# A 2:4-pruned matrix product on one core: the first weights in one load, and the order of the first x tiles

## The chip, the core and the metric

The kernel runs on one core of a Trainium2 chip. A core has five engines with instruction streams of their own: TensorE (PE in the profile, its weight loads PEld), VectorE (DVE), ScalarE (ACT), GpSimd (POOL) and SyncE (SP). Data comes in and goes out by DMA; here SyncE and ScalarE issue all transfers, each on a queue of its own, and the rows SPq and ACTq of the timeline are those issues. The metric is the time of one execution in microseconds on the device. Before the change the median of three runs was 232.76 us (232.62 to 232.90).

## The reference

```python
B, S, D = 16, 512, 1024            # x: B x S x D, w: D x D, b: D, all bfloat16
wg = w.reshape(D // 4, 4, D)
mag = jnp.abs(wg)
order = jnp.argsort(mag, 1)
thr = jnp.take_along_axis(mag, order[:, 2:3, :], 1)
mask = (mag >= thr).astype(w.dtype)
wp = (wg * mask).reshape(D, D)
return jnp.einsum("bsd,df->bsf", x, wp) + b
```

Of every four neighbouring weights of a column those below the second largest magnitude are set to zero; then 8192 rows of x are multiplied by the pruned 1024 x 1024 matrix and the bias is added.

## The kernel before

x has 64 tiles of 128 rows (t = 0 to 63). A product with TensorE needs x with the reduction along the partitions, that is, transposed. Most tiles come transposed from the DMA (`load_lead`, `load_low`, `load_nat`). For the first seven (NPK = 7) the lower half of the reduction (k below 512) is done otherwise, since at the start there is neither a pruned weight nor time to wait for one in its final layout:

- The weights are loaded with the four members of a pruning group side by side on one partition (`w_sb`, `load_w`, line 100), in six pieces (`pieces`, line 130): pieces 0 to 3 are 256 columns each of the first half of the rows (g = 0), pieces 4 and 5 are 512 columns each of the second.
- VectorE prunes a piece in steps (`Piece.do`, line 164): `abs`, the larger and smaller of pairs (`hi`, `lo`), the second largest (`t1`, `t2`, `thr`), `mask`, and the multiplication into `wp` (`mult`). Steps may be cut into parts; in the names of the order below, u, v, s, t are single members of the group, x and y pairs of them, p and q halves of the columns. `mult0yp` is thus the first quarter of piece 0 to be ready, `mult2t` a quarter of piece 2. For pieces 2 and 3 ScalarE takes over the `abs` step (`abs2`, `abs3`).
- The seven tiles of x come in natural layout (`load_x`, line 103: tiles 5-6, 3-4, 2 and 0-1, 512 columns each), are transposed on TensorE (`transpose`, line 188, the `T` names; matmuls of line 193) and copied out of PSUM by ScalarE (`copy_xt`, line 196, the `C` names).
- TensorE then multiplies them piece by piece (`mm_piece`, line 213, the `M` names: M3.0yp is tile 3 with the quarter yp of piece 0; line 229). Sums of finished pieces are staged in SBUF by ScalarE (`stage`, the `S` and `U` names).

Meanwhile `wp` is spread into the layout of the later products (`spread`, line 144, the `W` names, into `wp_nat`), four DMAs for each half of the columns and of the rows. Tiles 7 to 11 start on the lower half of k (`open_solo`, `open_nat`, names E and A), all twelve are closed with the upper half (`closes`, line 423, `close`, line 451), and the other 52 follow in seven batches (line 472), eight products for each half of the columns, VectorE adding the bias out of PSUM (`evac`, line 435) and ScalarE's queue storing.

The order on each engine is written by hand (`order`, line 266): `run` (line 391) takes each engine's names in turn, emitting one as soon as what it needs has been emitted, and `seq` fixes the order of emission on the engine. TensorE's list begins with

```python
"T3a T4a T5a T6a T2a M3.0yp M4.0yp M3.0yq M4.0yq M5.0y M6.0y M3.0u M4.0u ..."
```

so tiles 3 and 4 are transposed first, then 5 and 6, then 2, and the first product waits for `mult0yp`. VectorE's list begins with `abs0a abs0b` (two members of the group each) and goes through pieces 0 to 5 without anything else between. SyncE's list, `W0.0 Z W0.1 X1 W1.0p X2 Y1 Y0 W1.1`, mixes spreads with loads of weights, bias and transposed x.

Ahead of all this TensorE runs matmuls on constants whose result nobody reads (`filler`, line 136; called in lines 404 and 405): six of 512 columns and fourteen of 128.

The loads that open the kernel stand in lines 118 to 129. The first weights (piece 0, 256 KB) are split: members 0 and 1 on SyncE's queue, 2 and 3 on ScalarE's. Behind them ScalarE's queue loads x tiles 5-6, SyncE's x tiles 3-4, x tile 2, piece 1, x tiles 0-1 and the further weights. `LATE` (lines 46, 492 and 494) is the number of last tiles that are stored in two halves, each as soon as its half of the columns is done, rather than whole.

Of the kernel before, what the change touches and what calls it, by code (L numbers as in the profile page):

```python
# [11 lines left out]
def kernel(  # L12
# [30 lines left out]
    STG = 8  # L43
    SOLO = 6
    GROUPS = ((0, 3), (3, 6), (6, 7))
    LATE = 6
    sizes = (4, 8, 8, 8, 8, 8, 8)
    batches = []
    t0 = NPK + LEAD
# [23 lines left out]
    def pe(i):  # L73
        return seq("pe", i)
# [4 lines left out]
    def act(i):  # L79
        return seq("act", i)  # L80
# [15 lines left out]
    def issue(eng, out_, in_):  # L96
        q = nc.sync if eng == "sp" else nc.scalar
        return seq(eng, q.dma_start(out_, in_))

    def load_w(g, c0, c1, ma=0, mb=4, eng="sp"):  # L100
        issue(eng, w_sb[:, g, ma:mb, c0:c1], wv[:, g, ma:mb, c0:c1])

    def load_x(ta, tb, eng="sp"):
        xs = const.tile([P, tb - ta, HK], bf16, name=f"x_{ta}")
        issue(eng, xs[:], xf[ta * P:tb * P, :HK].rearrange("(t p) k -> p t k", p=P))
        for t in range(ta, tb):
            x_sb[t] = xs[:, t - ta, :]
# [7 lines left out]

    xnat, held = {}, {}

    load_w(0, 0, 256, 0, 2)
    load_w(0, 0, 256, 2, 4, "act")
    load_x(5, 7, "act")  # L120
    act(nc.scalar.activation(spark[:], nc.const_aps.tensor(1.0, [P, 1], bf16), Act.Abs))
    load_x(3, 5)
    load_x(2, 3)
    load_w(0, 256, 512)
    load_x(0, 2)
# [10 lines left out]
    def filler(n, rep=1):  # L136
        for _ in range(n):
            pe(nc.tensor.matmul(warm_ps[:, :rep * P], lhsT=nc.const_aps.tensor(1.0, [P, P], bf16),  # L138
                                rhs=nc.const_aps.tensor(1.0, [P, rep * P], bf16), start=True, stop=True))
# [251 lines left out]
    def run(queues):  # L391
        while any(queues.values()):
            moved = False
            for eng, toks in queues.items():
                while toks and all(n in written for n in needs(eng, toks[0])):
                    emit(eng, toks[0])
                    tok = toks.pop(0)
                    written.add(tok)
                    if tok[0] == "M" or tok[0].islower():
                        written.update(atoms(tok))  # L400
                    moved = True
            assert moved, queues

    filler(6, 4)
    filler(14)
    run({eng: order[eng].split() for eng in order})

    def load_nat(ta, tb):
# [26 lines left out]
    def evac(o, ps, c0, c1, add=None):  # L435
        if add is None:
            dve(nc.vector.tensor_tensor(o[:, c0:c1], ps, bias_sb[:, c0:c1], op=Alu.add))  # L437
        else:
            dve(nc.vector.tensor_tensor(o[:, c0:c1].rearrange("p (n c) -> p n c", n=2),  # L439
                                        ps.rearrange("p (n c) -> p n c", n=2), add, op=Alu.add))  # L440
# [4 lines left out]
    def store(eng, t, o, c0=0, c1=Dout):  # L445
        issue(eng, rows(t)[:, c0:c1], o[:, c0:c1])
# [25 lines left out]
    for bi, (tb, nb) in enumerate(batches):  # L472
        if bi:
            load_batch(bi + 1)
        for j in range(nb):
# [9 lines left out]
            else:  # L485
# [4 lines left out]
                for h in range(2):  # L490
                    evac(o, pss[h][:], h * FH, (h + 1) * FH)
                    if t >= NT - LATE:
                        store("act", t, o, h * FH, (h + 1) * FH)
                if t < NT - LATE:
                    store("act", t, o)
# [30 lines left out]
```

## Time and profile before

| | |
|---|---|
| median of the runs | 232.76 us |
| the profiled execution | 232.89 us |
| its span, first to last instruction | 231.1 us |
| TensorE busy | 226.6 us, 98% of the span |
| VectorE busy | 107.9 us, 47% |
| ScalarE busy | 14.0 us, 6% |
| GpSimd busy | 17.6 us, 8% |

Times in the rows count from the first instruction. A row of the timeline has start, duration, engine, line, operation, what is written and read, the shapes and the number of like instructions that were merged; in brackets the idle time ahead of it and what ended it. A merged row's duration runs to the end of its last instruction; matmuls and VectorE's operations overlap their neighbours a little. A line "DMA to landing" gives the time from the issue of a transfer until its data are in place. A row of the windows gives, after the busy times, the granted clock of TensorE, the mean busy share of the DMA engines and what they moved in GB/s.

### The profile page before, as it was taken

The page shows a single profiled execution, that of the slowest core. Times are in us where ns is not written, and L with a number is a line of the kernel's source. Part 1 is how long each engine was busy: PE and PEld are TensorE (multiplying, and loading weights), DVE is VectorE, ACT ScalarE, POOL GpSimd, SP SyncE. Part 2 cuts the span into 40 slices and gives each one's busy share as a digit, 9 for nine tenths or more (in the row PEclk, how much of TensorE's full clock was granted, in tenths as well). Part 3 has the DMA queues.
Part 4 walks back from the last instruction along what each step waited for, and adds up shares of the span by engine and source line. Part 5 has one row for each costly group of instructions (what it writes and reads, how often), then busy time and mean ns, then how long its engine had stood idle before and what let it go on. Part 6 is the DMA issues. An engine that isn't in the chain of part 4 may idle for free.

```text
span 231.1 us, 2851 instructions
## 1 busy us (share of the span) xinstructions
PE 226.6 (98%) x1142; PEld 110.9 (48%) x1162; DVE 107.9 (47%) x200; ACT 14.0 (6%) x27; POOL 17.6 (8%) x15
## 2 busy tenths in 40 slices
PE   8999999999999999999999999999999999999995
PEld 5986444444444444444444444444444444444443
DVE  3999877844424424424424424423423423433434
ACT  2874100000000000000000000000000000000000
POOL 1000199700000000000000000000000000000000
PEclk9999999999999999999999999999999999999999
DMA  6999999997399422991259821693128932122122
GB/s 203 276 197 280 164 217 223 297 320 252 124 206 232 155 91 72 237 281 64 75 116 252 222 94 71 162 298 134 65 91 198 273 122 83 54 91 91 53 86 91
DMA packets 79308, 38.19 MB, mean 165 GB/s; under 512 B 64192, under 2 KB 71744, under 8 KB 79296
## 3 DMA queue, kind: packets, MB, share of 16 engines
q1 hardware_dynamic: 68384, 20.75, 43.6%
q10 hardware_dynamic: 10912, 17.27, 20.9%
q8 instruction: 9, 0.15, 0.3%
q14 instruction: 3, 0.02, 0.0%
HBM read 3.28 MB, written 16.78 MB: 87 GB/s over the span
## 4 chain that ended last, share of the span: by engine, by line
PE 98%; issue 0%; DVE 0%
PE ps L242 88%; PE ps L229 5%; PE tp L242 2%; PE ps L138 2%; PE tp L193 1%; PE ps L193 0%; DVE o L437 0%
## 5 line engine op out<-in xcount | busy, mean ns | idle before, releaser
L242 PE MATMUL ps<-wp_nat,xb 128*128 128x512 bf16 (+1 forms) x831 | 178.9, 375 | 0.9
L242 PEld LDWEIGHTS <-xb 128*128 128x128 bf16 x848 | 82.2, 98 | 97.7
L437 DVE TENSOR_TENSOR o<-ps,bias_sb 128x512 bf16<-128x512 f32 (+1 forms) x112 | 71.6, 677 | 113.7 <-PE ps L242 111.4
L433 POOL TENSOR_TENSOR st<-st,bias_sb 128x1024 f32<-128x1024 f32 x8 | 16.7, 2142 | 0.0
L242 PE MATMUL ps<-wp_nat,xlead 128*128 128x512 bf16 x63 | 14.7, 379 | 0.1
L242 PEld LDWEIGHTS <-xlead 128*128 128x128 bf16 x88 | 8.6, 98 | 10.2
L229 PE MATMUL ps<-wp,xt 128*128 128x256 bf16 (+1 forms) x130 | 12.8, 258 | 0.0
L439 DVE TENSOR_TENSOR o<-ps,st 128x512 bf16<-128x512 f32 x16 | 11.1, 691 | 2.8 <-PE ps L242 2.2
L229 PEld LDWEIGHTS <-xt 128*128 128x128 bf16 x130 | 10.9, 98 | 1.1
L242 PE MATMUL ps<-wp_nat,xlow 128*128 128x512 bf16 x47 | 10.6, 379 | 0.1
L264 ACT COPY st<-ps 128x512 f32<-128x512 f32 x14 | 7.4, 600 | 3.2 <-PE ps L229 3.1
L242 PEld LDWEIGHTS <-xlow 128*128 128x128 bf16 x48 | 4.7, 98 | 5.7
L159 DVE TENSOR_TENSOR mag<-mag,hi 128x256 bf16<-128x256 bf16 (+2 forms) x15 | 6.1, 435 | 0.1
L159 DVE TENSOR_TENSOR wp<-w_sb,mag 128x256 bf16<-128x256 bf16 (+2 forms) x15 | 6.1, 435 | 0.1
L242 PE MATMUL tp<-wp_nat,xlead 128*128 128x512 bf16 x23 | 5.8, 380 | 0.0
L138 PE MATMUL ps<-const-bfloat16-1.0 128*128 128x128 bf16 (+1 forms) x20 | 4.2, 408 | 0.8 <-PEq L510 0.8
L169 DVE TENSOR_SCALAR mag<-w_sb 128x512 uint16<-128x512 uint16 (+2 forms) x5 | 2.3, 473 | 3.5 <-DMA w_sb<-in_w_dram 3.5
L138 PEld LDWEIGHTS <-const-bfloat16-1.0 128*128 128x128 bf16 x20 | 2.3, 146 | 2.4 <-issue 2.4
L159 DVE TENSOR_TENSOR hi<-mag 128x512 bf16<-128x512 bf16 (+2 forms) x7 | 3.2, 458 | 0.1
L159 DVE TENSOR_TENSOR lo<-mag 128x512 bf16<-128x512 bf16 (+1 forms) x6 | 3.1, 509 | 0.0
L193 PEld LDWEIGHTS <-x 128*128 128x128 bf16 x28 | 2.3, 124 | 0.3 <-DMA x<-in_x_dram 0.2
L422 POOL COPY pruned<-wp 128x1 bf16<-128x1 bf16 x1 | 0.2, 187 | 26.7 <-DVE wp L159 26.7
(18 smaller groups left out, 18.8 us busy)
## 6 DMA issues: line engine op xcount, KB each, us to landing
out_dram<-o ACTq DMA_DIRECT2D x58, 256.0 KB, 2.4
wp_nat<-wp SPq DMA_DIRECT2D x14, 128.0 KB, 3.2
out_dram<-o ACTq DMA_DIRECT2D x10, 128.0 KB, 1.7
w_sb<-in_w_dram SPq DMA_DIRECT2D x2, 512.0 KB, 5.5
w_sb<-in_w_dram SPq DMA_DIRECT2D x3, 256.0 KB, 5.1
x<-in_x_dram SPq DMA_DIRECT2D x2, 256.0 KB, 4.3
x<-in_x_dram ACTq DMA_DIRECT2D x1, 256.0 KB, 4.0
bias_sb<-in_b_dram SPq DMA_DIRECT2D x1, 256.0 KB, 4.7
```

Source lines behind the costliest of these rows:

```text
L138: pe(nc.tensor.matmul(warm_ps[:, :rep * P], lhsT=nc.const_aps.tensor(1.0, [P, P], bf16), rhs=nc.const_aps.tensor(1.0, [P, rep * P], bf16), ...
L159: dve(nc.vector.tensor_tensor(out, a, b_, op=op))
L169: dve(nc.vector.tensor_single_scalar(mag.bitcast(u16), w_.bitcast(u16), 0x7FFF, op=Alu.bitwise_and))
L193: pe(nc.tensor.transpose(tp[:, m, :], xg[:, m, :], ident[:]))
L229: pe(nc.tensor.matmul(ps[:, c0 + d:c1 + d], lhsT=xpk[t][:, m, :], rhs=wp[:, g, m, c0:c1], start=(new and m == ms.start), stop=(left[key] = ...
L242: pe(nc.tensor.matmul(ps, lhsT=xt[:, kt - koff, :], rhs=wp_nat[:, kt, c0:c1], start=(kt == first), stop=(kt == last)))
L264: act(nc.scalar.copy(staged[(q, h)][:, at, :, :].rearrange("p t c -> p (t c)"), ps_open.pop(key)[:]))
L422: pool(nc.gpsimd.tensor_copy(out=pruned[:], in_=wp[:, 1, 3, Dout - 1:]))
L433: pool(nc.gpsimd.tensor_tensor(st[:], st[:], bias.to_broadcast([P, 2, 2, CW]), op=Alu.add))
L437: dve(nc.vector.tensor_tensor(o[:, c0:c1], ps, bias_sb[:, c0:c1], op=Alu.add))
L439: dve(nc.vector.tensor_tensor(o[:, c0:c1].rearrange("p (n c) -> p n c", n=2), ps.rearrange("p (n c) -> p n c", n=2), add, op=Alu.add))
```

## The change

```diff
-    LATE = 6
+    LATE = 7
...
-    load_w(0, 0, 256, 0, 2)
-    load_w(0, 0, 256, 2, 4, "act")
-    load_x(5, 7, "act")
+    load_w(0, 0, 256)
+    load_x(3, 5, "act")
     act(nc.scalar.activation(spark[:], nc.const_aps.tensor(1.0, [P, 1], bf16), Act.Abs))
-    load_x(3, 5)
+    load_x(5, 7)
     load_x(2, 3)
     load_w(0, 256, 512)
...
     filler(6, 4)
-    filler(14)
+    filler(10)
```

The weights of piece 0 are loaded whole, in one transfer, as the first on SyncE's queue. x tiles 3-4 are the first and only opening transfer of ScalarE's queue; tiles 5-6 take their place on SyncE's, behind the weights and ahead of tile 2. What follows on SyncE's queue is unchanged. There are ten short fillers instead of fourteen. One more tile, 57, is stored in two halves. The order lists of the engines are the same; in the built program the instructions of TensorE, VectorE and ScalarE stand in the same order as before, except for those named, and lines after the loads move up by one.

## The prediction

> **What bounds the kernel now.** I read the page's summary first, then the chain of waits, then the first 5 us of the timeline, where all of the change but one line lies.
>
> ```profile
> span 231.1 us, 2851 instructions
> PEclk9999999999999999999999999999999999999999
> PE 98%; issue 0%; DVE 0%
> PE ps L242 88%; PE ps L229 5%; PE tp L242 2%; PE ps L138 2%; PE tp L193 1%; PE ps L193 0%; DVE o L437 0%
> ```
>
> The chain that ends last is TensorE from end to end. Once the products run, nothing but a hole in TensorE's own sequence makes the kernel longer, and only an earlier first product makes it shorter. L138 is the fillers, L193 the transposes of x, L229 the first products. So the question is when L229 starts, and whether it stalls after that.
>
> ```profile
> 0.73 0.45 SPq L98 DMA_DIRECT2D w_sb<-in_w_dram  x1
> 0.74 0.50 ACTq L98 DMA_DIRECT2D w_sb<-in_w_dram  x1
> 0.77 4.21 PE L138 MATMUL ps<-const-bfloat16-1.0 128*128 128x512 bf16 x20 [0.77 <-PEq L510]
> 1.24 0.96 SPq L98 DMA_DIRECT2D x<-in_x_dram  x2
> 1.26 0.49 ACTq L98 DMA_DIRECT2D x<-in_x_dram  x1
> 3.50 0.49 DVE L169 TENSOR_SCALAR mag<-w_sb 128x512 uint16<-128x512 uint16 x2 [3.50 <-DMA w_sb<-in_w_dram]
> 4.96 0.14 PEld L193 LDWEIGHTS <-x 128*128 128x128 bf16 x2 [0.24 <-DMA x<-in_x_dram]
> ```
>
> Today the two weight halves go out first, one on each queue; x 3-4 (SyncE) and x 5-6 (ScalarE) follow half a microsecond later. Two engines wait: VectorE until 3.50 for the weights, TensorE's weight load 0.24 us at 4.96 for x 3-4. What the waits are worth shows at the other end, where TensorE takes up what VectorE made. In the following rows of TensorE, by start, the last four are the first products of pieces 0, 1, 2 and 3:
>
> ```profile
> 3.29 1.70 PE L138 MATMUL ps<-const-bfloat16-1.0 128*128 128x128 bf16 x14
> 4.96 1.04 PE L193 MATMUL tp<-ident,x 128*128 128x128 bf16 x8
> 5.80 0.72 PE L193 MATMUL ps<-ident,x 128*128 128x128 bf16 x8
> 6.35 0.39 PE L193 MATMUL tp<-ident,x 128*128 128x128 bf16 x4
> 6.58 0.22 PE L229 MATMUL ps<-wp,xt 128*128 128x128 bf16 x1
> 10.09 0.39 PE L229 MATMUL ps<-wp,xt 128*128 128x128 bf16 x4
> 13.18 0.38 PE L229 MATMUL ps<-wp,xt 128*128 128x256 bf16 x2
> 16.24 0.38 PE L229 MATMUL ps<-wp,xt 128*128 128x256 bf16 x2
> ```
>
> and these are the multiplications on VectorE that they need (mult0yp, mult1yp, mult2t, mult3t):
>
> ```profile
> 5.80 0.28 DVE L159 TENSOR_TENSOR wp<-w_sb,mag 128x256 bf16<-128x256 bf16 x1
> 9.29 0.28 DVE L159 TENSOR_TENSOR wp<-w_sb,mag 128x256 bf16<-128x256 bf16 x1
> 12.49 0.28 DVE L159 TENSOR_TENSOR wp<-w_sb,mag 128x256 bf16<-128x256 bf16 x1
> 15.49 0.28 DVE L159 TENSOR_TENSOR wp<-w_sb,mag 128x256 bf16<-128x256 bf16 x1
> ```
>
> End of a multiplication to start of its product: 6.08 to 6.58, 9.57 to 10.09, 12.77 to 13.18, 15.77 to 16.24: 0.50, 0.52, 0.41 and 0.47 us. VectorE has no other wait from 3.50 to the last multiplication, so what its start loses, all four lose. It is half a microsecond ahead of TensorE four times over, and no more.
>
> **The change, part by part.** *The weights in one load.* Before, 256 KB of weights were all that the DMA engines had at first; after, the same 256 KB share them with 256 KB of x 3-4, sent at the same moment on the other queue. When they land is not in the trace; I work it out from what was moved.
>
> ```profile
> 1.50:2.00 0.50, 0.50 (x2) 0.15 (x1) 0.00 (x0) 0.21 (x1) 0.00 (x0) 1.00 0.11 27
> 2.00:2.50 0.50, 0.50 (x3) 0.22 (x2) 0.00 (x0) 0.50 (x1) 0.00 (x0) 1.00 0.56 151
> 2.50:3.00 0.50, 0.50 (x3) 0.22 (x2) 0.00 (x0) 0.50 (x1) 0.00 (x0) 1.00 1.03 302
> 3.00:3.50 0.50, 0.50 (x5) 0.23 (x4) 0.00 (x0) 0.28 (x2) 0.00 (x0) 1.00 0.82 275
> 3.50:4.00 0.50, 0.50 (x7) 0.50 (x6) 0.50 (x3) 0.00 (x0) 0.00 (x0) 1.00 1.09 389
> 4.00:4.50 0.50, 0.50 (x8) 0.50 (x6) 0.50 (x3) 0.00 (x0) 0.00 (x0) 1.00 1.10 383
> 4.50:5.00 0.50, 0.50 (x6) 0.26 (x5) 0.50 (x5) 0.00 (x0) 0.00 (x0) 1.00 1.08 357
> DMA to landing us min/median/max: 2.7/2.8/2.9
> ...
> DMA to landing us min/median/max: 4.0/4.0/4.0
> ```
>
> The last number of a window is GB/s; half of each, summed, gives 89 kB moved by 2.5 us, 240 by 3.0, 377 by 3.5, 572 by 4.0, 763 by 4.5. The two landing lines are of the weight halves and of x 5-6. Both halves (262 kB) are through at 3.0 + 22/275 = 3.08 and the later has landed at 0.74 + 2.9 = 3.64: 0.56 us on top. All four transfers (786 kB) are through at 4.56 and x 5-6 has landed at 1.26 + 4.0 = 5.26: 0.70 on top. Weights and x 3-4 together (524 kB) are through at 3.5 + 147/389 = 3.88. The two halves of today, on two queues, landed within 0.2 us of each other, so the queues share; of two equal loads sharing, the weights end with the pair: 3.88 + 0.56 = 4.44. VectorE would start at 4.45 instead of 3.50: 0.95 us later. Bounds: 0.14 (weights served before x, landing like the later half today, 3.64) and 1.46 (landing only at 4.96, when x 3-4 is taken up now). I take 0.95, since the one pair of loads in the trace that left together was shared.
>
> The Trainium skill (DMA: Bandwidth & Descriptors, section Queues, rings and completion order) says that each DMA engine goes round between the queue rows that have work, a packet at a time; two loads on two queues then end together. By that rule the start slips by the 0.95 us above; without sharing, by 0.14. The landings of the two halves agree with the rule.
>
> *From VectorE to TensorE.* One stretch of VectorE can shrink:
>
> ```profile
> 9.47 1.06 ACT L162 ACTIVATE mag<-w_sb 128x1024 bf16<-128x1024 bf16 x1
> 10.14 0.43 DVE L159 TENSOR_TENSOR wp<-w_sb,mag 128x512 bf16<-128x512 bf16 x1
> 10.56 0.43 DVE L159 TENSOR_TENSOR lo<-mag 128x512 bf16<-128x512 bf16 x1
> ```
>
> lo2 starts 0.03 us after ScalarE's abs2 ends (9.47 + 1.06 = 10.53); without that wait it would overlap the multiplication ahead of it by some 0.08, as the other independent neighbours do (mult0yp starts at 5.80 and mult0yq 0.20 later, each taking 0.28). A VectorE that comes 0.95 later doesn't wait there: 0.07 won back from piece 2 on. The 0.03 is also my price of a hand-over. The products then start at
> - piece 0: 6.08 + 0.95 + 0.03 = 7.06, 0.48 later than today's 6.58;
> - piece 1: 9.57 + 0.98 = 10.55, 0.46 later;
> - piece 2: 12.77 + 0.91 = 13.68, 0.50 later;
> - piece 3: 15.77 + 0.91 = 16.68, 0.44 later.
> The largest, 0.50, stays, since TensorE has no hole later in which to lose it.
>
> *x 3-4 first, 5-6 behind the weights, four fillers fewer.* A short filler takes (5.80 - 4.96)/8 = 0.105, the step of the cold transposes behind it. Ten end at 3.29 + 1.05 = 4.34 instead of 4.76, and x 3-4 lands by 4.44. x 5-6 ends the same 786 kB as today, so about 5.26; x 2 and the next weights likewise have as many bytes ahead of them as before. Transposes: 3 and 4 from 4.45, 5 and 6 from 5.3 at 0.105 each until the clock steps up, 2 after them: done by about 6.33, against 6.58. That gain of 0.25 us lies under the wait for mult0yp until 7.06, and so is worth nothing; if VectorE were early, it would be the whole gain. Conversely x 3-4 may land 0.7 us later than I say before it costs anything. SyncE's queue issues as many transfers as before, the first of them of double length, ScalarE's one fewer; the table load behind it on ScalarE comes earlier, and its first use, a copy of a transpose, not before 4.9.
>
> *What VectorE's delay moves behind it.* The spreads of finished weights on SyncE's queue wait for the multiplications, and transposing loads queue behind them. The last spread is the tightest:
>
> ```profile
> 30.04 2.49 SPq L98 DMA_DIRECT2D wp_nat<-wp  x4
> DMA to landing us min/median/max: 3.0/3.0/3.0
> 28.15 0.59 PE L242 MATMUL ps<-wp_nat,xlead 128*128 128x512 bf16 x2
> 31.38 7.07 PE ps L242 x32
> ```
>
> The fourth is issued at about 30.04 + 3/4 x 2.49 = 31.9 and has landed 3.0 later, at 34.9. The closings begin at 28.15 (third row) and take 7.07/32 = 0.22 a product (last row, of the chain of waits). The first reader of the fourth spread is the fortieth of them (nine closings of four, then the fourth product of the tenth): 28.15 + 39 x 0.22 = 36.7. 1.8 us of cover against 0.9: costs nothing; were the cover gone, the 0.9 would come in place of the 0.50.
>
> *LATE 7.* One more output tile leaves in two halves, about 20 us before the end, on a ScalarE queue that has nothing else to do: between 0 and the 0.3 us of an issue, hidden; I take 0.
>
> **Sum.** +0.50. The profiled execution took 232.89 us, its span 231.1 and 1.8 around it: 233.39, span 231.6. The median, 232.76, is 0.13 lower: 233.26. I say 233.3.
>
> **The rivals.** *A, the weights go first.* Place: the DMA engines between 1.8 and 3.9 us. If SyncE's transfer is served ahead of ScalarE's, VectorE is late by only 0.14; products start at 6.33, set by the transposes, and piece 2 at 12.77 + 0.14 + 0.03 = 12.94 or a little sooner, 0.24 earlier than 13.18. Gain 0.25: 232.5. It decides below a delay of about 0.45 us: there the kernel is not slower. For it: SyncE's issue starts a hair before ScalarE's (0.73, 0.74). Against it: the halves' landings.
>
> *B, the clock.* The page's clock row stays at 9, yet the steps of the transposes show a slow and a fast TensorE: 8 from 4.96 to 5.80 (0.105 each), 8 from 5.80 to 6.35 (0.069 on average), 4 from 6.35 to 6.58 (0.058). The step up falls at about 6.0, 5.25 us after the first filler. Four fewer fillers, and a wait of 0.7 us ahead of the first product, could put it off. Counted anew from 7.06, between the 1.06 us that it took from 4.96 and the 5.25 from the first filler would run at half pace, costing half of that, 0.5 to 2.6; the middle, 1.6, gives 234.9. Against it: fillers and transposes still leave no hole over 0.3 us up to 6.0. The Trainium skill (TensorE: Matmul & The Clock Gate, section Part 4: PE-mode transpose) has it that transposes don't count as activity for the clock; by that, fewer fillers would put the step off as in B. The trace agrees only in part: the step falls among transposes.
>
> *C, the change doesn't do what it says.* The two don't move at the same moment: x 3-4 takes the engines first and the weights land when x 3-4 is taken up today, at 4.96. VectorE is 1.46 late, the products 1.46 - 0.45 = 1.0: 233.8. Only the longer issue of SyncE's transfer speaks for it.
>
> **How the numbers follow.** Forecast 0.62, A 0.22, B 0.08, C 0.08. The time is the forecast's. Its own range, from a delay of 0.75 to 1.15 and 0.15 for the measurement, is 232.9 to 233.6. For 8 in 10 it goes down to 232.4 (A and a little) and up to 234.0 (C and the low end of B). 0.2% is 0.47 us, about what a measurement can tell from none: 232.3 and 233.2. Slower: all of B and C and some two thirds of the forecast, 0.58. Faster needs A and more than its 0.25: 0.06. The rest, 0.36, is within.
>
> **What would show it.** Right: VectorE's first row at 4.3 to 4.6; transposes at about 4.4; a wait of TensorE before the first product, ended by VectorE, and that product at 7.0 to 7.1; the first product of piece 2 at 13.6 to 13.7; 0.5 us more at every later point. Wrong: VectorE starting before 3.95 (A), the 0.105 us steps lasting past 7 us (B), VectorE after 4.8 (C), or a TensorE wait on a spread after 20 us.

## The result, and the profile after

The changed kernel takes 233.35 us (median of seven runs, 233.17 to 233.66); the kernel before took 232.51 beside it (seven runs, 232.40 to 232.90). The ratio is 1.0033, 95% interval 1.0024 to 1.0043: slower by 0.8 us. The profiled execution took 233.46 us, its span is 231.7.

First the chain of waits of the changed kernel, from its page:

```profile
span 231.7 us, 2864 instructions
PE 96%; DMA 2%; DVE 1%; issue 0%
PE ps L241 88%; PE ps L228 5%; PE tp L241 2%; DMA w_sb<-in_w_dram 2%; DVE hi L158 0%; DVE lo L158 0%; DVE mag L168 0%; DVE mag L158 0%; DVE o L436 0%; PE ps L192 0%; PE tp L192 0%; DVE wp L158 0%
```

Before, the chain was TensorE from end to end, fillers included (L138). Now it goes back from the first products to VectorE and from there to the load of the weights: 2% of 231.7 us is the time from the issue of that load to its landing, and the fillers are gone from the chain. One line of the page thus says what has changed: who holds the first product.

The timeline of the first 5 us of the changed kernel, and the times to landing of x 3-4, of the weights and of x 5-6 (in this order):

```profile
0.73 0.68 SPq L98 DMA_DIRECT2D w_sb<-in_w_dram  x1
0.74 0.43 ACTq L98 DMA_DIRECT2D x<-in_x_dram  x1
1.48 1.10 SPq L98 DMA_DIRECT2D x<-in_x_dram  x2
4.36 1.02 PE L192 MATMUL tp<-ident,x 128*128 128x128 bf16 x8
4.50 0.49 DVE L168 TENSOR_SCALAR mag<-w_sb 128x512 uint16<-128x512 uint16 x2 [4.50 <-DMA w_sb<-in_w_dram]
...
DMA to landing us min/median/max: 2.7/2.7/2.7
...
DMA to landing us min/median/max: 3.7/3.7/3.7
...
DMA to landing us min/median/max: 3.8/3.8/3.8
```

VectorE starts at 4.50, 1.00 later than before. But the two loads that left together didn't end together: x 3-4 landed at 0.74 + 2.7 = 3.4, and the weights a full microsecond behind it, at 4.4 to 4.5. TensorE had no use for x that early: its fillers ran on, and the first transpose came at 4.36.

TensorE's rows that answer to those of before, then VectorE's multiplications and the two operations around lo2:

```profile
5.28 0.64 PE L192 MATMUL ps<-ident,x 128*128 128x128 bf16 x8
5.75 0.39 PE L192 MATMUL tp<-ident,x 128*128 128x128 bf16 x4
7.13 0.27 PE L228 MATMUL ps<-wp,xt 128*128 128x128 bf16 x2 [0.99 <-DVE wp L158]
10.64 0.39 PE L228 MATMUL ps<-wp,xt 128*128 128x128 bf16 x4
13.75 0.50 PE L228 MATMUL ps<-wp,xt 128*128 128x256 bf16 x3
16.82 0.38 PE L228 MATMUL ps<-wp,xt 128*128 128x256 bf16 x2
19.88 0.59 PE L241 MATMUL tp<-wp_nat,xlead 128*128 128x512 bf16 x2
```

```profile
6.79 0.28 DVE L158 TENSOR_TENSOR wp<-w_sb,mag 128x256 bf16<-128x256 bf16 x1
10.28 0.28 DVE L158 TENSOR_TENSOR wp<-w_sb,mag 128x256 bf16<-128x256 bf16 x1
13.41 0.28 DVE L158 TENSOR_TENSOR wp<-w_sb,mag 128x256 bf16<-128x256 bf16 x1
16.41 0.28 DVE L158 TENSOR_TENSOR wp<-w_sb,mag 128x256 bf16<-128x256 bf16 x1
...
10.02 1.06 ACT L161 ACTIVATE mag<-w_sb 128x1024 bf16<-128x1024 bf16 x1
...
11.14 0.42 DVE L158 TENSOR_TENSOR wp<-w_sb,mag 128x512 bf16<-128x512 bf16 x1
11.48 0.42 DVE L158 TENSOR_TENSOR lo<-mag 128x512 bf16<-128x512 bf16 x1
```

The half microsecond between VectorE and TensorE is used up: 7.07 to 7.13, 10.56 to 10.64, 13.69 to 13.75, 16.69 to 16.82. TensorE finished its transposes at 6.14 (0.6 us before the old ones ended, at 6.74) and stood idle for 0.99. lo2 now starts 0.08 ahead of the end of the multiplication (11.56) and no longer waits for abs2 (11.08): the 0.07 that the prediction counted on. The first product of the next stage (L241) is at 19.88 against 19.30 in the profile of before, and the spans differ by the same: 231.7 against 231.1.

The 0.58 of the two profiles is less than the 0.8 of the medians. The first experiments below ask what the loss is made of, the last ones why the two numbers differ.

### The profile page after: what moved, and what is told of

Its sections match the earlier page's. It is cut to its first block, busy times and chain, and to the rows that moved or that the text cites. A ratio compares the mean times of both kernels' runs of the same rounds, so it can differ in the third digit from the quotient of the medians.

```text
span 231.7 us, 2864 instructions
## 1 busy us (share of the span) xinstructions
PE 227.2 (98%) x1158; PEld 110.5 (48%) x1158; DVE 107.8 (47%) x200; ACT 14.0 (6%) x27; POOL 17.6 (8%) x15
## 4 chain that ended last, share of the span: by engine, by line
PE 96%; DMA 2%; DVE 1%; issue 0%
PE ps L241 88%; PE ps L228 5%; PE tp L241 2%; DMA w_sb<-in_w_dram 2%; DVE hi L158 0%; DVE lo L158 0%; DVE mag L168 0%; DVE mag L158 0%; DVE o L436 0%; PE ps L192 0%; PE tp L192 0%; DVE wp L158 0%
## 5 line engine op out<-in xcount | busy, mean ns | idle before, releaser
L241 PE MATMUL ps<-wp_nat,xb 128*128 128x512 bf16 (+2 forms) x848 | 179.8, 375 | 0.0
L241 PEld LDWEIGHTS <-xb 128*128 128x128 bf16 x848 | 82.4, 98 | 97.5
L241 PE MATMUL ps<-wp_nat,xlead 128*128 128x512 bf16 x64 | 14.8, 379 | 0.0
L241 PEld LDWEIGHTS <-xlead 128*128 128x128 bf16 x88 | 8.6, 98 | 10.2
L241 PE MATMUL ps<-wp_nat,xlow 128*128 128x512 bf16 x48 | 10.7, 379 | 0.0
L241 PEld LDWEIGHTS <-xlow 128*128 128x128 bf16 x48 | 4.7, 98 | 5.7
L241 PE MATMUL tp<-wp_nat,xlead 128*128 128x512 bf16 x24 | 6.0, 379 | 0.0
```

Of the source, the lines that this page charges most:

```text
L241: pe(nc.tensor.matmul(ps, lhsT=xt[:, kt - koff, :], rhs=wp_nat[:, kt, c0:c1], start=(kt == first), stop=(kt == last)))
```

## The experiments

All kernels were run beside the kernel before; ratios are to that, with 95% intervals. Its median over these runs was 232.6 us.

**The parts of the change.** The loads alone, with fourteen fillers and LATE 6:

```diff
-    LATE = 7
+    LATE = 6
...
-    filler(10)
+    filler(14)
```

> The three edits of the loads alone; fourteen short fillers and LATE 6 as before the change. Theory (the weights land a microsecond later, because x 3-4 is sent at the same moment, and VectorE passes that on): VectorE starts at 4.5, the fillers end at 4.8, the transposes follow at once and still end before 6.6, the first product waits for VectorE until 7.1, and the ratio to before is that of the whole change, 1.0025 to 1.0045. Rival (the four missing fillers, by a later clock step, or the seventh split store): the loss is gone, ratio 0.999 to 1.001, first product at 6.6 or earlier.

233.44 us, ratio 1.0035 (1.0023 to 1.0047). VectorE started at 4.21, the transposes ran from 4.78 to 6.79, the first product came at 6.85, right behind `mult0yp`. The loads alone cost as much as the whole change. The expected times were 0.3 us too late, since the weights landed earlier here (4.19) than in the profile of the changed kernel (4.47).

The rest alone, in the kernel before:

```diff
-    LATE = 6
+    LATE = 7
...
-    filler(14)
+    filler(10)
```

> The loads of before; only ten fillers and LATE 7. Theory: VectorE at 3.5, TensorE waits for x 3-4 from 4.35 to 4.96, first product between 6.1 and 6.6 depending on when the clock steps up, ratio 0.999 to 1.001. Rival (fillers and store are the loss): ratio 1.0025 or more, the cold 0.105 us steps of the transposes lasting past 6.6, or the last tiles leaving later.

232.99 us, ratio 1.0010 (1.0000 to 1.0021), at the upper end of what the theory expected and below the rival's 1.0025. In the profile VectorE started at 3.40, and yet the first product came at 6.75, 0.76 after `mult0yp`: the transposes went at the slow step until 6.6. And the split store alone:

```diff
-    LATE = 6
+    LATE = 7
```

> Of the change only LATE 7. Theory: the split store is hidden, ratio 0.999 to 1.001. Rival (the 0.33 us by which the kernel with ten fillers, LATE 7 and the old loads stood above before come from the split store): ratio 1.001 to 1.002 with the last store landing later after TensorE's end.

232.61 us, ratio 1.0005 (0.9994 to 1.0016): no effect that can be told from none, so the 0.10% of the rest, if it is real, belongs to the fillers. It isn't settled that it is real, nor that fewer fillers put the fast step off: in the profiles with ten fillers it came between 4.7 and 6.7, in those with fourteen between 3.6 and 6.3 (one kernel with ten, in which it came at 9.8, follows below).

**Why the weights land late.** The changed kernel with `load_x(3, 5)` on SyncE's queue, everything else equal:

```diff
     load_w(0, 0, 256)
-    load_x(3, 5, "act")
+    load_x(3, 5)
```

> The changed kernel with one edit: x 3-4 behind the weights on SyncE's queue instead of beside them on ScalarE's, so that every opening load is on one queue in the order weights, 3-4, 5-6, 2. Theory (a transfer whose issue ends first is served first, and the weights, whose issue takes 0.68 us, lost their place to x 3-4, whose issue takes 0.43): nothing overtakes the weights, VectorE starts at 3.4 to 3.8, x 3-4 lands at 4.2 to 4.6, first product at 6.1 to 6.4, ratio to before 0.998 to 1.000. Rival (one load on one queue is slow whatever stands beside it): VectorE at 4.1 or later, first product at 6.7 or later, ratio 1.001 or more.

232.93 us, ratio 1.0022 (1.0004 to 1.0040), neither as good nor as bad as expected. From the profile, VectorE's first row, the weights' time to landing, the first product and the first of L241:

```profile
3.84 0.49 DVE L168 TENSOR_SCALAR mag<-w_sb 128x512 uint16<-128x512 uint16 x2 [3.84 <-DMA w_sb<-in_w_dram]
...
DMA to landing us min/median/max: 3.1/3.1/3.1
...
6.47 1.92 PE L228 MATMUL ps<-wp,xt 128*128 128x128 bf16 x20
...
19.22 1.03 PE L241 MATMUL tp<-wp_nat,xlead 128*128 128x512 bf16 x4
```

With nothing beside it, the single load landed 3.1 us after its issue instead of 3.7. So of the one microsecond that VectorE lost, about two thirds (4.50 to 3.84) is what x 3-4 took away, and the last third (3.84 to 3.50) is the single load itself: the halves landed 2.7 and 2.9 us after their issue. The issue on SyncE's queue took 0.68 us for the whole load and 0.45 for a half. The 3.50 is the latest start in six profiles with the loads of before; in the other five VectorE started between 3.33 and 3.40, and against those the single load itself costs nearer 0.5 us.

The trace also records every DMA packet (here one run in memory, 512 B of weights or 1 KB of x) with its queue: q1 is SyncE's, q10 ScalarE's. These moved from 1.5 to 2.75 us, first in the changed kernel, then in `all_sp`, then in the kernel before:

```profile
q10 hardware_dynamic: 193, 0.20, 45.3%
...
q1 hardware_dynamic: 187, 0.10, 28.8%
...
q1 hardware_dynamic: 232, 0.12, 35.1%
q10 hardware_dynamic: 97, 0.05, 13.1%
```

In the changed kernel 193 of the 256 packets of x 3-4 had gone by then and none of the weights: their first packet went at 2.81, against 2.20 in `all_sp`, and these 0.61 us are nearly all of the 0.66 between the two starts of VectorE. So x 3-4 went first and the weights behind it. The engines were not full meanwhile: the packets of x took 45.3% of their time. The halves of the kernel before (first packets at 1.83 and 2.29) did overlap, with SyncE's ahead.

The other attempt to leave the weights alone failed in an instructive way. x 5-6 was put on ScalarE's queue behind the table load, to be sent late:

```diff
-    load_x(3, 5, "act")
     act(nc.scalar.activation(spark[:], nc.const_aps.tensor(1.0, [P, 1], bf16), Act.Abs))
-    load_x(5, 7)
+    load_x(5, 7, "act")
+    load_x(3, 5)
```

> The weights whole on SyncE's queue as in the change, but nothing beside them: x 3-4 follows on SyncE's queue, and x 5-6 goes on ScalarE's queue behind the table load. Ten fillers, LATE 7. Theory (what delays the weights is the transfer sent with them, not that they are one load on one queue): VectorE starts at 3.4 to 3.7, x 3-4 lands at 4.2 to 4.5, first product at 6.1 to 6.4, ratio 0.998 to 1.000. Rival (one queue alone moves the 256 KB too slowly, or its longer issue is the delay): VectorE starts at 4.0 or later, first product at 6.7 or later, ratio 1.001 or more.

234.83 us, ratio 1.0087 (1.0069 to 1.0105). ScalarE's rows, TensorE's transposes, its first twenty products, and five of these:

```profile
0.74 1.28 ACT L119 ACT_TABLE_LOAD   x1 [0.74 <-PEq L509]
0.80 0.43 ACTq L98 DMA_DIRECT2D x<-in_x_dram  x1
...
5.35 1.04 PE L192 MATMUL tp<-ident,x 128*128 128x128 bf16 x8 [0.79 <-DMA x<-in_x_dram]
...
7.46 3.07 PE L228 MATMUL ps<-wp,xt 128*128 128x128 bf16 x20
...
8.74 1.25 PE L228 MATMUL ps<-wp,xt 128*128 128x256 bf16 x5
```

The load was issued at 0.80, while the table was still loading: the table load doesn't hold the queue. So x 5-6 went out beside the weights, these landed at 4.55 as in the changed kernel, and x 3-4, now third, left TensorE idle for 0.79 us. As a test of the theory it says nothing beyond a second case of a load beside the weights. But it shows the loss that rival B of the prediction describes, a fast step that comes late: the twenty products that took 1.92 us in the kernel `all_sp` above took 3.07 here; the five of the last row, of 256 columns, are among them and lie 0.21 us apart, against 0.11 at the fast step. The fast step came at 9.8, and the first product of L241 at 21.34.

Does the order in which issues end decide who is served first? x 2 behind x 3-4 on ScalarE's queue, in the changed kernel:

```diff
     load_x(3, 5, "act")
+    load_x(2, 3, "act")
...
     load_x(5, 7)
-    load_x(2, 3)
```

> The changed kernel with x 2 moved from SyncE's queue to ScalarE's, behind x 3-4. Theory (served in the order in which the issues end): the issue of x 2 ends at about 1.65, after that of the weights at 1.42, so the weights stay second: VectorE at 4.3 to 4.6 as in the changed kernel, ratio to before 1.002 to 1.004. Rival (the queues share the engines, as the prediction had it): 128 KB more go beside the weights, which land 0.3 us later: VectorE at 4.7 to 4.9, ratio 1.004 to 1.006.

234.07 us, ratio 1.0070 (1.0043 to 1.0098); times to landing of x 3-4, x 2 and the weights:

```profile
DMA to landing us min/median/max: 3.0/3.0/3.0
...
DMA to landing us min/median/max: 3.9/3.9/3.9
...
DMA to landing us min/median/max: 4.5/4.5/4.5
```

x 2, issued at 1.20, landed at 1.20 + 3.9 = 5.1, ahead of the weights issued at 0.73 (5.2; VectorE at 5.28), so the theory of the issue order falls. The delay of 0.78 against the changed kernel is also more than twice what 128 KB more beside the weights were to cost, so equal sharing has the direction and not the size. In the packet record the weights' packets begin at 2.79, as in the changed kernel; x 2's go from 3.63 to 4.49 among the second half of the weights', the last of which went at 4.54 instead of 4.05. And the two first loads with their queues exchanged:

```diff
-    load_w(0, 0, 256)
-    load_x(3, 5, "act")
+    load_w(0, 0, 256, eng="act")
+    load_x(3, 5)
```

> The changed kernel with the two first loads on each other's queue: the weights whole on ScalarE's, x 3-4 first on SyncE's. Theory (the load whose issue ends first goes first, and the weights' issue is the longer on either queue): x 3-4 lands at 3.3 to 3.6, the weights at 4.2 to 4.6, VectorE as late as in the changed kernel, ratio to before 1.002 to 1.004. Rival (ScalarE's queue is served ahead of SyncE's): the weights land at 3.4 to 3.8, x 3-4 at 4.4, first product 6.1 to 6.5, ratio 0.998 to 1.001.

233.63 us, ratio 1.0036 (1.0023 to 1.0049): x 3-4 on SyncE's queue landed at 3.5, the weights on ScalarE's at 4.5, VectorE at 4.56. Neither queue is favoured; in both places the load of x came out a microsecond ahead of the weights, whose first packet went at 2.81 and 2.85. What rule makes it so stays open. The two differ in three things that weren't separated: the length of the issue (0.43 to 0.45 against 0.66 to 0.68 us), the length of a run in memory (1 KB against 512 B), and the number of runs (256 against 512).

**In search of a better order.** Two kernels keep the halves of before and change what follows. Tile 3 on SyncE's queue and tile 4 on ScalarE's, ahead of 5-6 (against the kernel before, which also gets LATE 7 and ten fillers):

```diff
     load_w(0, 0, 256, 2, 4, "act")
+    load_x(3, 4)
+    load_x(4, 5, "act")
     load_x(5, 7, "act")
...
-    load_x(3, 5)
```

> The weights in two halves on two queues as before the change, and behind them tile 3 on SyncE's queue, tile 4 on ScalarE's, then 5-6 on ScalarE's. Ten fillers, LATE 7. Theory: VectorE at 3.5, and x 3-4 ahead of 5-6 on both queues lands at 4.2 to 4.5 instead of 4.9; transposes from 4.4, first product as soon as VectorE lets it, 6.1 to 6.3, whenever the clock steps up; ratio 0.998 to 1.000, 232.3 to 232.5 us. Rival (more and smaller transfers cost more than they bring): tile 3 or 4 lands after 4.9, first product at 6.6 or later, ratio 1.000 or more.

Halves, and then all of x on SyncE's queue (against the changed kernel):

```diff
-    load_w(0, 0, 256)
-    load_x(3, 5, "act")
+    load_w(0, 0, 256, 0, 2)
+    load_w(0, 0, 256, 2, 4, "act")
+    load_x(3, 5)
```

> The weights in halves on the two queues as before the change; then on SyncE's queue alone x 3-4, 5-6 and 2, so that 5-6 is behind 3-4 instead of beside it. Ten fillers, LATE 7. Theory: weights as before, VectorE at 3.3 to 3.5; x 3-4 lands at 4.1 to 4.4 instead of 4.9, x 5-6 at 5.1 to 5.3 as before; first product as soon as VectorE lets it, 6.0 to 6.3; ratio 0.997 to 0.9995. Rival (the clock of TensorE steps up later when there are fewer fillers, as the run with the old loads and ten fillers hints): cold transposes to the end, first product at 6.4 to 6.8, ratio 1.000 to 1.002.

The first took 233.42 us (1.0037, 1.0023 to 1.0052), the second 233.32 (1.0030, 1.0012 to 1.0047). In both VectorE started early, at 3.30 and 3.56, and x 3-4 landed at 4.2 to 4.6, about as expected; but a later transfer came late. From the first, VectorE's row for piece 1 and the time to landing of its weights, and from the second the transposes of tiles 5 and 6:

```profile
7.99 0.43 DVE L170 TENSOR_SCALAR mag<-w_sb 128x1024 uint16<-128x1024 uint16 x1 [1.10 <-DMA w_sb<-in_w_dram]
...
DMA to landing us min/median/max: 5.8/5.8/5.8
```

```profile
6.59 0.64 PE L193 MATMUL ps<-ident,x 128*128 128x128 bf16 x8 [1.11 <-DMA x<-in_x_dram]
```

Piece 1 took 5.8 us to land in the one, x 5-6 4.8 in the other, about a microsecond more than in the kernel before (4.5 and 4.0). Why these transfers were slow, with the same bytes ahead of them, isn't known. Neither kernel, nor any other tried, beats the kernel before.

**Why the medians differ by more than the profiles.** The kernel before, without any edit, profiled twice more:

> The kernel before, profiled once more. Theory (in the profile shown, 232.89 us, TensorE was late by itself, since the clock stepped up only at 6.0; in the faster executions it steps up earlier and the first products are held by VectorE alone): if this execution takes 232.3 to 232.6 us, the cold 0.105 us steps end before 5.9 and the first product of a tile 7 (line 242) comes 15.4 us after VectorE's start, as in the changed kernel; if it takes 232.8 or more, the cold steps last to 6.0 or longer and it comes 15.7 us or more after it. Rival (the fast executions differ elsewhere, in the stages after the products of line 229): the first product of line 242 comes at 19.3 whatever the time.

> The kernel before, profiled a third time; expected as for the second.

The second execution took 232.37 us, the third 232.65. Rows of the second: VectorE's start, transposes, first product, first product of L242.

```profile
3.36 0.56 DVE L169 TENSOR_SCALAR mag<-w_sb 128x512 uint16<-128x512 uint16 x2 [3.36 <-DMA w_sb<-in_w_dram]
...
4.70 0.64 PE L193 MATMUL tp<-ident,x 128*128 128x128 bf16 x8 [0.29 <-DMA x<-in_x_dram]
5.17 0.61 PE L193 MATMUL ps<-ident,x 128*128 128x128 bf16 x8
5.62 0.39 PE L193 MATMUL tp<-ident,x 128*128 128x128 bf16 x4
6.06 1.92 PE L229 MATMUL ps<-wp,xt 128*128 128x128 bf16 x20
...
18.81 1.03 PE L242 MATMUL tp<-wp_nat,xlead 128*128 128x512 bf16 x4
```

Eight transposes go from 4.70 to 5.17, at 0.058 us each. The fast step was there before them, since 3.6, among the fillers; these are rows of the short fillers, first of this execution, then of the one that the prediction was made from:

```profile
3.72 0.63 PE L138 MATMUL ps<-const-bfloat16-1.0 128*128 128x128 bf16 x8
...
3.50 0.63 PE L138 MATMUL ps<-const-bfloat16-1.0 128*128 128x128 bf16 x4
```

and this is `mult0yp` of the second execution:

```profile
5.73 0.28 DVE L159 TENSOR_TENSOR wp<-w_sb,mag 128x256 bf16<-128x256 bf16 x1
```

The first product follows it at once (6.01 to 6.06), and L242 begins at 18.81 instead of 19.30, 15.45 us after VectorE's start. In the third execution VectorE started at 3.33, the fast step came at 5.7, the first product 0.42 after `mult0yp`, and L242 at 19.08, 15.75 after VectorE's start. So the lead of VectorE that the prediction read is there in two of the three profiles of this kernel, and in the second it is gone: with the early step VectorE holds TensorE already in the kernel before. The step has the size for it, since nine or ten transposes at 0.107 instead of 0.056 us make 0.5 us. The profile that the prediction was made from (232.89 us, against a median of 232.5) was late on both sides: its fast step came at 6.0, and its first loads landed late, VectorE starting 0.14 and 0.17 after the other two and the transposes 0.26 and 0.18.

A last one, sixteen fillers and the loads of before, leaves no hole ahead of the transposes:

```diff
-    filler(14)
+    filler(16)
```

> The kernel before with sixteen short fillers, so that they end at about 4.98 and leave no hole ahead of the transposes. Theory (the moment at which the clock steps up varies from execution to execution on its own, and a hole of 0.2 us doesn't move it): ratio 0.9995 to 1.0005, same spread as before. Rival (a hole in TensorE's work puts the step off): without it the step comes earlier, ratio 0.997 to 0.999 and times near 232.4.

232.50 us, ratio 0.9994 (0.9984 to 1.0005), times from 232.25 to 233.13 as widely spread as those of before; in its profile the fast step came at 6.0 though there was no hole. That is the theory's result, but an effect of up to 0.16% isn't excluded.

All profiles side by side, in the order of the last column (times in us from the span's start; the last column is the distance from VectorE's start to the first product of the next stage):

| kernel | VectorE starts | first product | next stage (L241 to L243) | distance |
|---|---|---|---|---|
| loads alone | 4.21 | 6.85 | 19.59 | 15.38 |
| the change | 4.50 | 7.13 | 19.88 | 15.38 |
| all on SyncE's queue | 3.84 | 6.47 | 19.22 | 15.38 |
| queues exchanged | 4.56 | 7.19 | 19.93 | 15.38 |
| x 2 on ScalarE's queue too | 5.28 | 7.92 | 20.66 | 15.38 |
| before, second profile | 3.36 | 6.06 | 18.81 | 15.45 |
| before, third | 3.33 | 6.36 | 19.08 | 15.75 |
| LATE 7 alone | 3.34 | 6.37 | 19.09 | 15.75 |
| before, first profile | 3.50 | 6.58 | 19.30 | 15.80 |
| sixteen fillers | 3.36 | 6.57 | 19.29 | 15.93 |
| rest alone | 3.40 | 6.75 | 19.47 | 16.07 |
| halves, then x | 3.56 | 7.29 | 20.01 | 16.45 |
| tiles 3 and 4 apart | 3.30 | 6.46 | 19.87 | 16.57 |
| x 5-6 beside the weights | 4.57 | 7.46 | 21.34 | 16.77 |

Wherever VectorE alone holds TensorE after the change, the distance is 15.38, over a range of 1.4 us in VectorE's start; in the second profile of before it is 15.45, since VectorE's first two operations took 0.56 there (row above) and 0.49 after the change. From the next stage to the end of the span it is 211.8 to 212.0 in every profile. What VectorE loses at its start beyond its margin, the kernel loses whole.

## Why the prediction was right

**The place and the sign: right.** The first weights land later, VectorE starts later, its lead over TensorE is spent, and the rest arrives at the end undiminished. Predicted for the changed kernel: VectorE at 4.45, first product at 7.06, piece 2 at 13.68, span 231.6; measured 4.50, 7.13, 13.75, 231.7. The hand-over took 0.06 where the prediction had 0.03. The 0.07 won back at lo2 was there. TensorE's early transposes were worth nothing, as forecast: they ended 0.99 us ahead of need.

**How the weights come to land at 4.4: right number, wrong mechanism.** The prediction had two equal loads share the engines and end together. They ended a microsecond apart, x 3-4 first. The packet record has the weights' first packet at 2.81, about a microsecond after x's first (1.83). The bytes of both had to pass before the weights were complete, which is why the sum 3.88 + 0.56 held for the weights (rival C's order with the forecast's time); for x 3-4 it was a microsecond too late. The halves of before, which the prediction took as proof of sharing, overlapped only in part (first packets 1.83 and 2.29), and their landings 0.2 us apart couldn't tell. The Trainium skill (DMA: Bandwidth & Descriptors, section Queues, rings and completion order) has an engine drain a whole packet of one queue, typically 9 to 17 descriptors, before it switches; that two loads end together was the prediction's conclusion from it and not the page's. If each of the 256 runs of x 3-4 is one descriptor, each of the 16 engines has 16 of them (an estimate), which may be a single such turn; that this is the reason for the order here isn't shown. The kernel with x 2 added shows that the sum by bytes is no law either: 0.3 us were due and 0.78 came.

**Rival A, the weights first:** didn't occur in the changed kernel. When nothing stood beside them (`all_sp`), VectorE was late by 0.34 against the 3.50 of the first profile, below the 0.45 at which the prediction put break-even, and that one profile has indeed a span of 231.0 against 231.1. Against the usual start of 3.33 to 3.40 it was late by 0.44 to 0.51, and the median is 0.3 us above before.

**The size: two terms too favourable, and the time met by luck.** Between the two profiles the loss is 0.58 for a forecast of 0.50: VectorE's delay was 1.00 and not 0.95, and the hand-over 0.06 and not 0.03. Between the medians it is 0.84. The profiled execution of before was 0.38 above its median, that of the changed kernel 0.11 above. Against the second and the third profile of before, between whose times (232.37 and 232.65) the median of 232.51 lies, the changed kernel reaches the next stage 1.07 and 0.80 later. Of what this is over 0.58, VectorE's earlier start makes 0.14 and 0.17, the shorter distance 0.35 and 0.05. So the delay of 0.95 was counted from a start that was late by itself; and the lead, the term "0.50, 0.52, 0.41 and 0.47", is right for the execution it was read from, 0.40 to 0.46 in the third and 0.05 to 0.12 in the second, where the fast step came at 3.6. Which of the two is the more frequent three profiles can't say. That 233.3 was forecast and 233.35 measured is luck: a loss taken 0.34 too small was added to 232.76, the median of the first three runs, which is 0.25 above that of seven.

**Rival B, the clock:** not in the changed kernel (fast step at about 5.4, under cover of the wait). In the kernel with x 5-6 beside the weights the fast step came only at 9.8, and the loss over the distance of 15.38 was 1.4 us, close to the 1.6 of the prediction. That the hole of 0.79 put it off is not shown: with halves and then all of x on SyncE's queue TensorE had a hole of 1.11 up to 6.59, and the fast step was there right behind it. Single runs of 235.2 to 235.7 in three other kernels with a hole in TensorE's start may be the same; they weren't profiled. The Trainium skill (TensorE: Matmul & The Clock Gate, section Part 4: PE-mode transpose) has it that the fast clock doesn't engage for transposes, which don't count as activity in the same way. It does engage here: behind the step, transposes ran at 0.056 us each, in most profiles from the middle of a row of them. Whether they count towards the step stays open, since fillers ran ahead of them in every profile.

**The later stages and LATE 7: right.** No wait of TensorE appears after the first product in the changed kernel; the spreads were in time.

## What to carry to other kernels

When two engines run in step, read the lead of the one over the other at every hand-over, in more than one execution: the smallest lead is all that a change may spend, and a single profile in which the waiting engine was late for another reason overstates it. Read the start that a delay is counted from in more than one execution too: here it was 3.50 in one and 3.33 to 3.40 in five others. Before sending a second load at the same moment as the one that everything waits for, ask who needs it first: here x came a microsecond early, to an engine that couldn't use it, at the expense of the weights. And a fast start of the engine with the longest chain (VectorE, whose 15.38 us no kernel here shortened) is worth more than an early start of the one that waits for it.

## What the runs showed of the hardware that was not expected

- The step to TensorE's fast clock isn't seen in the granted clock (1.00 throughout); it shows in the distance of like matmuls (0.107 against 0.056 us). Fillers began at 0.77 or 0.78 in all fourteen profiles, and it came between 3.6 and 6.7 us in thirteen of them, at 9.8 in one; in three executions of the same kernel at 3.6, 5.7 and 6.0.
- Of two 256 KB loads sent within 10 ns of each other on two queues, the one with longer runs and the shorter issue landed 1.0 us ahead, on either queue. No packet of the other moved before 2.81 and 2.85, though alone its first went at 2.20.
- A plain load of 256 KB, the first of its queue, took 0.43 to 0.45 us to issue as 256 runs of 1 KB and 0.66 to 0.68 as 512 runs of 512 B.
- ScalarE's queue issues a load while its engine's table load is still running (0.80 within 0.74 to 2.02).
